# Gate and up projections: the bank Y begins with a copy of the bank X made by ScalarE; first tiles, roots and units with sums of W in another order

## The chip, the cores and the metric

One core of a Trainium2 chip. The core has TensorE (PE, matrix products into eight PSUM banks; PEld is its loading of weights), VectorE (DVE), ScalarE (ACT), GpSimd (POOL), and queues of transfers (all of them issued by SyncE, SP). Each engine works through its own list of instructions in the order in which the program was written for it, and waits at an instruction until its operands are there and its destination is free. The metric is the time of one execution in microseconds (us); less is better.

## The reference

A pre-norm block: Fourier mixing as two matrix products, and a gated feed-forward part. One batch, S = 2048 tokens, D = 448, F = 1792, everything fp32.

```python
def _A_ref(x, dft_seq_re, dft_seq_im, dft_hid_re, dft_hid_im):
    a = jnp.einsum("bsd,ed->bse", x, dft_hid_re)
    b = jnp.einsum("bsd,ed->bse", x, dft_hid_im)
    y = jnp.einsum("ts,bse->bte", dft_seq_re, a) - jnp.einsum("ts,bse->bte", dft_seq_im, b)
    return y
def _B_ref(x, w_gate, w_up, w_down):
    g = jnp.einsum("bsd,df->bsf", x, w_gate)
    u = jnp.einsum("bsd,df->bsf", x, w_up)
    h = _gelu(g) * u
    return jnp.einsum("bsf,fd->bsd", h, w_down)
h = x + _A_ref(_layernorm(x, axis=-1), ...)
h2 = h + _B_ref(_layernorm(h, axis=-1), ...)
```

## The kernel before

**Precision.** Every fp32 operand of a product is split into a high and a low fp16 part: ACT rounds the high part (`hi_part`, L100), DVE takes the difference (`lo_part`, L106, or L104 where nothing is scaled). Three products (high by high, high by low, low by high) then add up in PSUM. So behind each operand stands the pair "ACT high part, then DVE low part", and PE needs both.

**Fewer products.** Where it can, the kernel forms 2x2 blocks with seven products in place of eight (Strassen's and Winograd's forms). The sums of blocks that this needs are made ahead by DVE or POOL, and the results are joined on the way out of PSUM.

**Stage 1, features (to 107 us).** Sixteen tiles of 128 tokens. `x_load` reads two tiles (224 KB each); `x_stats` takes mean and variance on DVE and, in the same step, the square root on ACT (`root`, L121); `x_rstd` and `x_bias` finish the factor on DVE; `x_norm` and `x_lo` write the normalised tile in two parts `xs`. Tiles 0 to 3 are turned by PE into a PSUM tile `xT_ps` (L370, seven transposes in pieces of four and three) that ACT copies out (L371); the others by a DMA. `feature_mm` (L408) multiplies a turned tile with the hidden weights (`wh_hi`, `wh_lo`, made from four pieces `wh_raw` of 448 KB) in 11 steps of two products of 448 columns. `feature_out` empties the two banks `ab` into `b`; for tiles 10 to 15 (units 5 to 7), ACT copies to fp32 (`b32`), POOL makes sums (L448) and the split follows.

**Stage 2, sequence (to 371 us).** 8 passes, each of 8 units of W (512 KB, `seq_load`). A plain unit takes 24 products of 448 columns (L494), its split 1024 columns by 128 rows on ACT and on DVE. Units 5, 6 and 7 are "units with sums" (`S_UNITS`): 42 products of 224 columns, seven parts of W in place of four, of which four are sums that DVE makes (`seq_sums`). Pass 0 is woven into stage 1. Between the passes stand `seq_out` (L520 to L528: the four banks and x added up to h, on DVE), the moments of h, a root, the normalisation (on ACT) and the splits for stage 3; and through all passes run the sums and splits of the 14 gate/up weights (`gu_w`), which are stored for stage 3.

The order of stages 1 and 2 is a list of slots, one for each tile of features or unit of a pass; `plan(n, rank, step)` puts a step ahead of the products of slot n, and within a slot the steps go by rank. The first tiles, up to the first slot, are written out by hand.

**Stage 3, feed-forward (to 700 us).** 56 tiles `GateUp`: four groups q of 512 tokens by 14 blocks f of gate and up columns, 128 wide, each with 256 columns of moving operand. A tile makes seven products in three banks X, Y, Z (39 instructions of 256 columns, L872). Here `A`, `B`, `S`, `T` are blocks and sums of blocks of the weights and of the normalised h. X takes `A11 B11`, then `A12 B21`; Y takes `S2 T2`, then `S3 T3`, then `A22 T4`; Z takes `S1 T1`, then `S4 B22`. Y doesn't hold `A11 B11`, so ACT copies X to SBUF as `u1` (L910) before X's second product, and DVE adds it at each reading of Y:

```python
A.activation(self.u1, self.X, AF.Copy, scale=SC)
plus(self.u2, self.Y, self.u1)      # after S2 T2
plus(u3, self.Y, self.u1)           # after S3 T3
plus(c21, self.Y, self.u1)          # after A22 T4
G.tensor_mul(c21, c21, self.g1)     # POOL: times gelu of X
```

`plus` (L882) is one DVE instruction from PSUM. Two more join Z with `u3` and `u2`; the second gives `c12`, whose Gelu (`c_last`, ACT L946, then a product on POOL, L948) comes a tile later. In group 0 there is no down projection, and the tiles take X, Y, Z and the free banks `a0` to `a2` by turns; the down weights are prepared meanwhile (`down_prep`: load, sums on POOL at L198 and L201, `down_hi` on ACT, `down_lo` on DVE). From group 1 on each tile carries 21 products of 224 columns of the down projection (`dn_mm`, L815), for an earlier group's hidden values, which are summed (`dn_sums`, POOL L965 and L966 and one on DVE) and split (`dn_split`, L100 and L104 into `dn_w`) first. The banks `a0` to `a3` then hold its sums, and one bank (`ps_tr`) is free until the end. Steps that go beside a tile (normalisation of groups 2 and 3, draining of the down banks, the root of the last block of h at tile 25) hang on a table `side`, entry (tile, place).

**Stage 4, tail.** The down products of the last group (`last_mm`).

Of the kernel before, what the change touches and what calls it, by code (L numbers as in the profile page):

```python
# [13 lines left out]
P = 128  # L14
# [18 lines left out]
def kernel(  # L33
# [143 lines left out]

    def ffn_rstd(q, j):
        tag = f"h{q}_{j}"
        mv = moments[q, j]  # L180
        moments[q, j] = mv, rstd(mv, root(mv, tag), tag, const)

    def ffn_stats(q, j, h):
        for g in range(2):
            ffn_moments(q, j, h, g)
        ffn_rstd(q, j)
# [123 lines left out]
    def x_stats(*tiles):  # L310
# [6 lines left out]
        norm_x[tiles] = mv, root(mv, tag)  # L317
# [14 lines left out]
    def x_norm(i):  # L332
        mv, r, g, *nb = norm_x.pop(i)
# [11 lines left out]
        hi_part(xs[i][:, 0:D], xn)  # L345
# [17 lines left out]
    ptr = {}  # L363

    def x_turn_pe(i, k0, k1):
        if k0 == 0:
            xT_tile(i)
            ptr[i] = ps_dft.tile([P, 8, P], F16, tag="A", name=f"xT_ps{i}")
        for k in range(k0, k1):
            PE.transpose(ptr[i][:, k, :], xs[i][:, k * P : (k + 1) * P], ident)  # L370
        A.activation(xT[i][:, k0:k1, :], ptr[i][:, k0:k1, :], AF.Copy)  # L371
# [219 lines left out]
    for n, s in enumerate(S_UNITS):  # L591
        mixed.insert(1 + n * 8 // len(S_UNITS), s)
# [33 lines left out]
    for g, (p, u) in enumerate(units):  # L626
# [3 lines left out]
        plan(n - 2 if g else -3, 3, lambda p=p, u=u: seq_split(p, u))  # L630
        if g < 4:
            plan((-6, -5, 1, 2)[g], 9, lambda p=p, u=u: seq_load(p, u))
# [22 lines left out]
    for p in range(N_PASS):  # L655
# [6 lines left out]
        plan(n + 1, 5, lambda q=q, j=j: ffn_stats(q, j, hp[q, j]))  # L662
# [12 lines left out]
    x_load(0, (slice(0, 1),))  # L675
    x_load(0, (slice(1, 2),))
    for k in range(4):
        wh_load(k)
    x_load(1)
    x_load(ORDER[2])  # L680
    x_stats(0)
    x_rstd(0)
    x_norm(0)
    wh_high(0)
    x_stats(1)
    x_lo(0)
    x_turn_pe(0, 0, 4)
    wh_high(1)
    wh_high(3, G)
    x_turn_pe(0, 4, 7)  # L690
    x_rstd(1)
    x_norm(1)
    wh_high(2)
    x_lo(1)
    wh_low(3, G)
    feature_mm(0, range(6))
    x_stats(2)
    x_turn_pe(1, 0, 4)
    x_turn_pe(1, 4, 7)
    feature_mm(0, range(6, 7))  # L700
# [3 lines left out]
    wh_low(0)  # L704
# [3 lines left out]
    feature_mm(1, range(4, 7))  # L708
    x_stats(3)
    wh_low(1)  # L710
# [4 lines left out]
    a, b = tiles_of[2]  # L715
    x_stats(a, b)
    x_rstd(a, b)
    x_bias(a, b)
    feature_mm(2, range(7), "A")
# [409 lines left out]
    for t in range(N_GU):  # L1129
# [19 lines left out]
        if t > 0:  # L1149
            if q == 0:  # L1150
                prev.c12_plus()
# [106 lines left out]
```

## Time and profile before

| | |
|---|---|
| time of three executions | 736.61, 738.90, 739.53 us; median 738.9 |
| the profiled execution | 736.13 us, of which the span of the profile is 734.3 |
| TensorE's granted clock | 0.998 of full speed |
| busy: PE, DVE, ACT, POOL | 97%, 79%, 44%, 36% of the span |
| matmuls | 5800 |
| moved by DMA | 142.9 MB |

The span is the time from the first to the last instruction that the profile shows. A row of the profile's groups names line, engine and operation, then destination and sources by the program's names; a chain or a list of waits gives beside an instruction, in brackets, how long its engine had been idle before it and which instruction ended that. "Start to start" below means the step from one product's start to the next one's; 448 columns take 0.19 us and 256 columns 0.109 us that way when nothing is late, while the row's own duration (0.3 and more) counts the pipeline behind it.

### The profile page before, as it was taken

To read this page: it belongs to the slowest core of one execution; us is meant where nothing else is said; L and a number is where in the kernel's file an instruction comes from. 1 tells how busy PE (TensorE), PEld (TensorE's weight loads), DVE (VectorE), ACT (ScalarE), POOL (GpSimd) and SP (SyncE) were. 2 spreads that over 40 slices of the span, in tenths; PEclk is the share of its full clock that TensorE was granted. 3 is DMA by queue.
4 is the path that set the end of the run, shared out by engine and by line. 5 is a ranking of instruction groups with operands and counts; after the bars stand their busy time and mean duration, and the time that the engine had idled before them with its cause. 6 is when DMAs were issued, how large, how long until landed. Compare 5 with 4: busy or idle time off the path is not lost.

```text
span 734.3 us, 14677 instructions
## 1 busy us (share of the span) xinstructions
PE 712.6 (97%) x5800; PEld 560.9 (76%) x5800; DVE 577.6 (79%) x1166; ACT 322.0 (44%) x624; POOL 265.7 (36%) x294
## 2 busy tenths in 40 slices
PE   7899999999999999999999989999999999999998
PEld 4455567676656566676778869999999999999998
DVE  5767849998989899999457788788787877989730
ACT  5556545445454545344234444345444334454310
POOL 4032140000000000020018886576676776858430
PEclk9999999999999999999999999999999999999999
DMA  8363345798878889686147745655648476565401
GB/s 320 91 156 80 79 149 172 255 234 259 240 266 241 271 238 304 235 319 200 69 167 266 277 170 177 189 182 173 180 147 232 172 217 224 181 222 202 151 14 63
DMA packets 72340, 142.90 MB, mean 195 GB/s; under 512 B 41296, under 2 KB 47568, under 8 KB 72272
## 3 DMA queue, kind: packets, MB, share of 16 engines
q1 hardware_dynamic: 72272, 141.97, 60.8%
q8 instruction: 45, 0.74, 0.4%
q14 instruction: 23, 0.19, 0.1%
HBM read 112.46 MB, written 20.19 MB: 181 GB/s over the span
## 4 chain that ended last, share of the span: by engine, by line
PE 65%; DVE 19%; ACT 7%; DMA 4%; issue 4%; POOL 2%; SPq 1%; ACTq 0%; DVEq 0%; POOLq 0%
PE acc L494 19%; PE pY L872 13%; PE acc_d L815 11%; PE pX L872 8%; PE pZ L872 8%; DVE ws L106 4%; DVE xs L104 2%; ACT ws L100 2%; DMA w_dram<-gu_w 2%; DVE gu_w L106 2%; ACT b L100 2%; DMA x<-in_x_dram 1%; PE last_Z L1035 1%; PE last_X L1035 1%; PE last_tr L1035 1%
## 5 line engine op out<-in xcount | busy, mean ns | idle before, releaser
L494 PE MATMUL acc<-b,ws 128*128 128x448 f16 (+1 forms) x1968 | 281.5, 305 | 4.5 <-DVE ws L106 4.4
L494 PEld LDWEIGHTS <-ws 128*128 128x128 f16 x1968 | 189.4, 98 | 96.0 <-DVE ws L106 9.6
L872 PEld LDWEIGHTS <-gw 128*128 128x128 f16 x2067 | 201.8, 98 | 25.9 <-issue 5.0
L872 PE MATMUL pY<-hops,gw 128*128 128x256 f16 x901 | 122.7, 273 | 4.2 <-DVE u L882 3.9
L815 PE MATMUL acc_d<-wd,dn_w 128*128 128x224 f16 x882 | 105.1, 259 | 0.0
L815 PEld LDWEIGHTS <-dn_w 128*128 128x128 f16 x882 | 85.1, 98 | 2.8
L198 POOL TENSOR_TENSOR wd_s<-wd 128x448 f32<-128x448 f32 x7 | 8.0, 1144 | 217.0 <-DMA wd<-in_w_down_dram 217.0
L106 DVE SCALAR_TENSOR_TENSOR ws<-wr,ws 128x1024 f16<-128x1024 f32 (+2 forms) x88 | 74.6, 871 | 14.8 <-ACT ws L100 14.2
L100 ACT ACTIVATE ws<-wr 128x1024 f16<-128x1024 f32 (+2 forms) x88 | 63.7, 756 | 49.3 <-issue 30.3
L872 PE MATMUL pX<-hops,gw 128*128 128x256 f16 x583 | 81.0, 273 | 0.0
L872 PE MATMUL pZ<-hops,gw 128*128 128x256 f16 x583 | 79.2, 273 | 0.0
L939 POOL TENSOR_TENSOR hh<-hh,g 128x256 f32<-128x256 f32 x42 | 36.8, 876 | 100.5 <-DVE hh L882 100.5
L882 DVE SCALAR_TENSOR_TENSOR u<-pY,u 128x256 f32<-128x256 f32 x112 | 47.0, 420 | 32.0 <-ACT c L946 15.9
L408 PEld LDWEIGHTS <-xT 128*128 128x128 f16 x352 | 34.6, 99 | 34.3 <-issue 3.9
L910 ACT ACTIVATE u<-pX 128x256 f32<-128x256 f32 x56 | 21.4, 382 | 86.3 <-PE pX L872 80.7
L104 DVE TENSOR_TENSOR dn_w<-dn_s,dn_w 128x640 f16<-128x640 f32 x42 | 52.7, 1255 | 1.6 <-ACT dn_w L100 1.4
L923 ACT ACTIVATE g<-pX 128x256 f32<-128x256 f32 x56 | 21.3, 380 | 70.5 <-PE pX L872 64.8
L408 PE MATMUL ab<-wh_hi,xT 128*128 128x448 f16 x224 | 46.5, 359 | 1.7 <-DVE b L106 1.7
L100 ACT ACTIVATE ws<-wsum 128x1024 f16<-128x1024 f32 x24 | 25.3, 1053 | 45.6 <-DVE wsum L468 45.6
L966 POOL TENSOR_TENSOR dn_s<-hh 128x256 f32<-128x256 f32 x42 | 43.9, 1046 | 0.0
L948 POOL TENSOR_TENSOR hh<-hh,c 128x256 f32<-128x256 f32 x42 | 37.3, 887 | 17.4 <-ACT c L946 17.4
L965 POOL TENSOR_TENSOR dn_s<-hh 128x256 f32<-128x256 f32 x42 | 42.4, 1010 | 0.0
(130 smaller groups left out, 932.3 us busy)
## 6 DMA issues: line engine op xcount, KB each, us to landing
gw<-w_dram SPq DMA_DIRECT2D x53, 896.0 KB, 4.7
wr<-in_w_seq_dram SPq DMA_DIRECT2D x64, 512.0 KB, 4.3
w_dram<-gu_w SPq DMA_DIRECT2D x14, 896.0 KB, 7.4
gu_raw<-in_w_gu_dram SPq DMA_DIRECT2D x28, 384.0 KB, 5.3
wd<-in_w_down_dram SPq DMA_DIRECT2D x14, 448.0 KB, 4.9
hx<-in_x_dram SPq DMA_DIRECT2D x8, 448.0 KB, 6.3
h_dram<-hx SPq DMA_DIRECT2D x8, 448.0 KB, 6.4
hr<-h_dram SPq DMA_DIRECT2D x8, 448.0 KB, 5.3
```

Source lines behind the costliest of these rows:

```text
L100: A.activation(dst, src, AF.Copy, scale=scale)
L104: V.tensor_sub(dst, src, hi)
L106: V.scalar_tensor_tensor(dst, src, scale, hi, op0=ALU.mult, op1=ALU.subtract)
L408: PE.matmul(feat[i][r][:, :D], xT[i][:, kx, :], w[:, kw, r * D : (r + 1) * D], start=n == 0, stop=n == 10,)
L494: PE.matmul(banks[k][:, cols], lhs, rhs, start=k not in begun, stop=stop, skip_group_check=True)
L815: PE.matmul(acc[k // 2][:, k % 2 * HD : (k % 2 + 1) * HD], a_of(la, a), b_of(lb, b), start=first and m == 0 and k % 2 == 0, stop=last and ...
L872: PE.matmul(ps, w[:, wl, wa + ws, :], ops[:, m + ms, :], start=first and n == 0, stop=last and n == len(terms) - 1, skip_group_check=True,)
L882: V.scalar_tensor_tensor(dst, ps, SC, other, op0=ALU.mult, op1=ALU.add)
L939: G.tensor_mul(c21, c21, self.g1)
L948: G.tensor_mul(c22, c22, self.c12)
L965: G.tensor_add(s[:, 0:2], t[:, 0:2], t[:, 2:4])
L966: G.tensor_sub(s[:, 2:4], t[:, 1:4:2], t[:, 0:4:2])
```

## The change

In five parts. No product is added or taken away.

(a) First tiles: the first hidden weight is loaded ahead of the second tile of x; the scaling of `wh_hi` 1 goes to DVE, that of `wh_hi` 3 from POOL to ACT; each of the two pieces of a turned tile gets its own PSUM tile; the products, turns and splits stand in another order. The load and the split of the first unit of W are placed by hand.

(b) `x_stats` no longer takes the root; `x_root` does, one slot later and ahead of the steps of higher rank. Likewise `ffn_root` and `ffn_rstd` stand one slot behind the moments. On ACT, in the first pass, around the root of tiles 6 and 7 (`sd_x6`), before:

```order
L100 ACTIVATE xs6_545<-x6_417 128x448
L121 ACTIVATE sd_x6_594<-mv_x6_587,eps_t_79 128x2
L100 ACTIVATE b32_11_622<-ab11_0_598 128x448
L100 ACTIVATE b32_11_622<-ab11_1_599 128x448
L100 ACTIVATE b10_626<-b32_10_575 128x1568
L100 ACTIVATE b11_664<-b32_11_622 128x1568
```
After:

```order
L100 ACTIVATE xs6_549<-x6_421 128x448
L100 ACTIVATE b32_11_624<-ab11_0_600 128x448
L100 ACTIVATE b32_11_624<-ab11_1_601 128x448
L121 ACTIVATE sd_x6_628<-mv_x6_591,eps_t_79 128x2
L100 ACTIVATE b10_630<-b32_10_579 128x1568
L100 ACTIVATE b11_668<-b32_11_624 128x1568
```
`ab11` to `b32_11` is the emptying of tile 11's two banks; it stood behind the root and stands ahead of it now. `xs6` is the high part of tile 6, `b10` and `b11` are the splits.

(c) Units with sums come at places 2, 5 and 7 of a pass, counted from 0, in place of 1, 3 and 6: the order of the units was 0, 5, 1, 6, 2, 3, 7, 4 and is 0, 1, 5, 2, 3, 6, 4, 7. On DVE, at the start of pass 2, around the moments of the second block of h (`st_h0_1`, `mv_h0_1`), before:

```order
L175 BN_STATS st_h0_1_0_1809<-hx1_1475 128x6
L176 BN_AGGR mv_h0_1_1808<-st_h0_1_0_1809 128x2
L175 BN_STATS st_h0_1_1_1812<-hx1_1475 128x6
L176 BN_AGGR mv_h0_1_1808<-st_h0_1_1_1812 128x2
L128 RECIPROCAL r_h0_1_1817<-sd_h0_1_1815 128x2
L129 TENSOR_SCALAR r_h0_1_1817<-mv_h0_1_1808 128x2
L130 TENSOR_TENSOR r_h0_1_1817<-r_h0_1_1817 128x2
L131 TENSOR_TENSOR r_h0_1_1817<-r_h0_1_1817 128x2
L132 SCALAR_TENSOR_TENSOR r_h0_1_1817<-r_h0_1_1817 128x2
L106 SCALAR_TENSOR_TENSOR gu_w10_1766<-gu_s10_1716,gu_w10_1766 128x512 x2
L106 SCALAR_TENSOR_TENSOR ws2_2_1875<-wr2_2_1662,ws2_2_1875 128x1024
```
After:

```order
L175 BN_STATS st_h0_1_0_1805<-hx1_1449 128x6
L176 BN_AGGR mv_h0_1_1804<-st_h0_1_0_1805 128x2
L175 BN_STATS st_h0_1_1_1808<-hx1_1449 128x6
L176 BN_AGGR mv_h0_1_1804<-st_h0_1_1_1808 128x2
L106 SCALAR_TENSOR_TENSOR gu_w10_1766<-gu_s10_1698,gu_w10_1766 128x512 x2
L106 SCALAR_TENSOR_TENSOR ws2_3_1847<-wr2_3_1662,ws2_3_1847 128x1024
L128 RECIPROCAL r_h0_1_1850<-sd_h0_1_1845 128x2
L129 TENSOR_SCALAR r_h0_1_1850<-mv_h0_1_1804 128x2
L130 TENSOR_TENSOR r_h0_1_1850<-r_h0_1_1850 128x2
L131 TENSOR_TENSOR r_h0_1_1850<-r_h0_1_1850 128x2
L132 SCALAR_TENSOR_TENSOR r_h0_1_1850<-r_h0_1_1850 128x2
```
Between the moments and the factor that needs the root (L128) stand now a low part of a gate/up weight (`gu_w10`) and of a plain unit (`ws2_3`); before, that low part of `gu_w10` and the next plain unit's (`ws2_2`) came behind it.

(d) Gate/up. After `A11 B11`, ACT copies X into the bank Y (`x_open`), and `S2 T2`, `S3 T3` and `A22 T4` add onto it. So `u2` and `u3` are plain scaled copies on ACT, and the last reading of Y is one DVE instruction that multiplies with `g1`, without POOL. Odd tiles of the later groups take `ps_tr` for Y; X of the next tile is begun inside the present one. `dn_sums` of the second block comes two tiles earlier, and the first `dn_split` behind tile 12's additions. On ACT, in tiles 12 and 13, before:

```order
L946 ACTIVATE c12_11_4870<-c12_11_4870 128x256
L100 ACTIVATE dn_w0_4874<-hh0_4101 128x256
L100 ACTIVATE dn_w0_4874<-dn_s0_4742 128x640
L923 ACTIVATE g1_12_4890<-pX_12_4828 128x256
L910 ACTIVATE u1_13_4909<-pX_13_4895 128x256
L946 ACTIVATE c12_12_4939<-c12_12_4939 128x256
L923 ACTIVATE g1_13_4958<-pX_13_4895 128x256
L910 ACTIVATE u1_14_4977<-pX_14_4963 128x256
```
After:

```order
L946 ACTIVATE g1_12_4860<-pX_12_4798 128x256
L932 ACTIVATE pY_13_4869<-pX_13_4862 128x256
L970 ACTIVATE c12_11_4844<-c12_11_4844 128x256
L951 ACTIVATE u3_12_4879<-pY_12_4805 128x256
L937 ACTIVATE u2_13_4895<-pY_13_4869 128x256
L100 ACTIVATE dn_w0_4910<-hh0_4111 128x256
L100 ACTIVATE dn_w0_4910<-dn_s0_4778 128x640
L946 ACTIVATE g1_13_4927<-pX_13_4862 128x256
L932 ACTIVATE pY_14_4936<-pX_14_4929 128x256
L970 ACTIVATE c12_12_4908<-c12_12_4908 128x256
```
`u1` is gone; `pY_13<-pX_13` and `pY_14<-pX_14` are the copies of X, and `u2`, `u3` are new here. The first split of the down projection (`dn_w0`) stood ahead of `g1_12` and stands now behind `u2_13`.

(e) The root of the last block of h stays at tile 25, and its factor moves to tile 27. The banks of the last products come in another order.

The diff, cut to its core:

```diff
@@ roots, first tiles
+    def ffn_root(q, j):
+        moments[q, j] = moments[q, j], root(moments[q, j], f"h{q}_{j}")
...
-        norm_x[tiles] = mv, root(mv, tag)
+        norm_x[tiles] = mv
+
+    def x_root(*tiles):
+        norm_x[tiles] = norm_x[tiles], root(norm_x[tiles], f"x{tiles[0]}")
...
-            ptr[i] = ps_dft.tile([P, 8, P], F16, tag="A", name=f"xT_ps{i}")
+        t = ps_dft.tile([P, 8, P], F16, tag="A", name=f"xT_ps{i}_{k0}")
...
@@ slots
-    for n, s in enumerate(S_UNITS):
-        mixed.insert(1 + n * 8 // len(S_UNITS), s)
+    for n, s in zip((2, 5, 7), S_UNITS):
+        mixed.insert(n, s)
...
+                plan(n - 6, 2, lambda i=i, j=i2: x_root(i, j))
...
-        plan(n + 1, 5, lambda q=q, j=j: ffn_stats(q, j, hp[q, j]))
+        for g in range(2):
+            plan(n + 1, 5, lambda q=q, j=j, g=g: ffn_moments(q, j, hp[q, j], g))
+        plan(n + 2, 2, lambda q=q, j=j: ffn_root(q, j))
+        plan(n + 2, 5, lambda q=q, j=j: ffn_rstd(q, j))
...
@@ first tiles, by hand
     x_load(0, (slice(0, 1),))
+    wh_load(0)
     x_load(0, (slice(1, 2),))
...
+    seq_load(0, ORDER[0])
...
-    x_norm(0)
+    x_norm_v(0)
     wh_high(0)
+    x_high(0)
...
-    wh_high(1)
-    wh_high(3, G)
+    wh_high(1, V)
...
-    feature_mm(0, range(7, 11))
-    feature_out(0)
-    feature_mm(1, range(7, 9))
-    x_turn_pe(3, 0, 4)
-    x_turn_pe(3, 4, 7)
-    feature_mm(1, range(9, 11))
+    x_turn_pe(3, 0, 4)
+    x_turn_pe(3, 4, 7)
+    feature_mm(0, range(8, 11))
...
+    feature_out(0)
...
+    feature_mm(1, range(8, 11))
...
@@ class GateUp
+            self.banks = [(ps_dn, f"a{k}") for k in range(3)] if self.q == 0 and odd else [(ps_gu, k) for k in "XYZ"]
+            if self.q and odd:
+                self.banks[1] = ps_tr, "tr"
...
-    def open(self):
-            self.mul(self.Y, "S2", "T2", True)
-            A.activation(self.u1, self.X, AF.Copy, scale=SC)
-            plus(self.u2, self.Y, self.u1)
+        def x_open(self):
+            self.X = self.bank(0)
             self.mul(self.X, "A11", "B11", True)
+            self.Y = self.bank(1)
+            A.activation(self.Y, self.X, AF.Copy)
+
+        def y_open(self):
+            self.mul(self.Y, "S2", "T2", False)
             self.u2 = ftile("u2", 2, f"u2_{self.name}")
+            A.activation(self.u2, self.Y, AF.Copy, scale=SC)
...
-            plus(u3, self.Y, self.u1)
+            A.activation(u3, self.Y, AF.Copy, scale=SC)
             plus(self.hidden(1), self.Z, u3)
...
-            plus(c21, self.Y, self.u1)
-            G.tensor_mul(c21, c21, self.g1)
+            V.scalar_tensor_tensor(self.hidden(0), self.Y, SC, self.g1, op0=ALU.mult, op1=ALU.mult)
...
@@ the tiles
-        if t in (NF - 4, NF - 1):
-            dn_sums(int(t == NF - 1))
+        if t in (NF - 4, NF - 3):
+            dn_sums(t - NF + 4)
...
-    at(side, (25, 4), lambda: ffn_rstd(NB - 1, 1))
+    at(side, (25, 4), lambda: ffn_root(NB - 1, 1))
+    at(side, (27, 1), lambda: ffn_rstd(NB - 1, 1))
...
         if q == 0:
+            cur.x_close()
+            nxt.x_open()
+            if prev:
+                prev.c_last()
+            cur.y_mid()
+            nxt.z_open()
+            nxt.y_open()
+            cur.y_close()
+            cur.z_close()
             dn_ahead(t)
...
+        else:
+            do(t, 0)
+            prev.c_last()
+            cur.x_close()
+            if t > NF:
+                cur.z_open()
+            if d + 1 < 6 * NC:
+                dn_split(d + 1)
+            dn_mm(d, range(0, 8))
+            cur.y_mid()
+            dn_ahead(t)
+            dn_mm(d, range(8, 18))
+            if nxt:
+                nxt.x_open()
+            do(t, 1)
+            do(t, 4)
+            cur.y_close()
+            cur.z_close()
+            dn_mm(d, range(18, 21))
+            do(t, 5)
+            if nxt:
+                nxt.y_open()
...
```

More of the change, by code (lines that the diff above doesn't have):

```diff
@@ L176, in ffn_moments @@
         V.bn_aggr(moments[q, j][:, g, :], st)
+    def ffn_root(q, j):
+        moments[q, j] = moments[q, j], root(moments[q, j], f"h{q}_{j}")
     def ffn_rstd(q, j):
[L179 to L186, printed above, removed]
+        mv, sd = moments[q, j]
+        moments[q, j] = mv, rstd(mv, sd, f"h{q}_{j}", const)
     wd32, wd_s = {}, {}
@@ L707 @@
     x_turn_pe(2, 4, 7)
[L708 removed]
+    feature_mm(1, range(4, 8))
     x_stats(3)
[L710 removed]
+    x_root(3)
     wh_low(2)
```

117 lines of the change are left out of this document (53 added, 64 removed).

## The prediction

> **What bounds the kernel now.** First the page's totals, then the waits of TensorE (PE), then the stretches in which they fall.
>
> ```profile
> span 734.3 us, 14677 instructions
> PE 712.6 (97%) x5800; PEld 560.9 (76%) x5800; DVE 577.6 (79%) x1166; ACT 322.0 (44%) x624; POOL 265.7 (36%) x294
> PE xT_ps L370 <- ACT xT L371: 5.8, 4, 2.3
> PE pY L872 <- DVE u L882: 4.5, 4, 2.3
> PE acc L494 <- DVE ws L106: 4.4, 10, 0.7
> 107.47 34.25 PE acc L494 x243
> 376.05 1.20 PE pZ L872 x11
> 600.00:640.00 40.00, 40.00 (x385) 37.20 (x384) 32.40 (x61) 16.48 (x40) 29.16 (x34) 1.00 0.59 203
> ```
>
> The second line is busy time by engine. The next three are PE's waits (sum, times, longest); then come two dense pieces of the chain and one stretch (length; busy of PE, PEld, DVE, ACT, POOL; clock; DMA). PE is the bound, and the change leaves its products as they are in number and size. So nothing can be won but PE's gaps, some 18 us behind the first 14, and the rows say where they are not: from 600 to 640 PE issues 385 products in 40 us without a hole, and 11 gate/up products take 1.20 (0.109 each). A gate/up tile has 39 of them, 4.26 us.
>
> **The change part by part.** The sum is made against the profiled execution: 736.13 us, 1.8 more than its span. The median of the runs, 738.9, is 0.38% above it, and I scale by that at the end.
>
> *(a) First tiles.*
>
> ```profile
> x<-in_x_dram SPq DMA_DIRECT2D x2, 224.0 KB, 2.7
> wh_raw<-in_w_hid_dram SPq DMA_DIRECT2D x4, 448.0 KB, 6.8
> 7.48 0.95 ACT L100 ACTIVATE wh_hi<-wh_raw 128x896 f16<-128x896 f32 x1 [0.97 <-DMA wh_raw<-in_w_hid_dram]
> 15.00 1.08 DVE L106 SCALAR_TENSOR_TENSOR wh_lo<-wh_raw,wh_hi 128x896 f16<-128x896 f32 x1
> 22.22 0.69 DVE L104 TENSOR_TENSOR xs<-x,xs 128x64 f16<-128x64 f32 x2 [0.64 <-ACT xs L100]
> 23.40 0.39 PE L370 MATMUL xT_ps<-ident,xs 128*128 128x128 f16 x4
> 24.63 0.96 ACT L100 ACTIVATE b<-ab 128x448 f16<-128x448 f32 x2
> 26.13 0.33 PE L370 MATMUL xT_ps<-ident,xs 128*128 128x128 f16 x3 [2.34 <-ACT xT L371]
> 32.72 3.57 PE L494 MATMUL acc<-b,ws 128*128 128x448 f16 x18
> ```
>
> At 26.13 PE has waited 2.34: the last three transposes of tile 3 share a PSUM tile with the first four, whose copy stands on ACT behind both copies of `b` (24.63). Now they have their own tile, and the copies stand ahead of `b`. Against this, `wh_hi` 0 stands ahead of tile 0's high part on ACT, and the second half of x queues behind 448 KB. That weight landed at 7.48; I let it land at 6.7 and the half of x at 7.3. DVE gets one scaling of `wh_hi` more: no row has it; a low part of that size takes 1.08 and half of it is the other end; I take 1.0, since the low part is the same read with one input more. I follow DVE's queue from there (moments 0.85, low part 0.7, scaling 1.0, and so on): tile 3's low part ends at 22.7 as now (22.22 and 0.69), its transposes start at 22.8, and behind them PE has only work that is ready: 42 products by 0.19 and seven transposes, 8.3. The first sequence product moves from 32.72 to 31.1: **-1.6**. Ends: -2.2 (the weights land as fast as the first x halves) and +0.5 (tile 2 comes 2 us late). The load of the first `wr`, two issues earlier on SP, costs nothing: its split is not due before 28.
>
> *(b) Roots in the first pass.*
>
> ```profile
> 49.23 0.29 ACT L121 ACTIVATE sd_x<-mv_x,eps_t 128x2 f32<-128x2 f32 x1 [2.71 <-DVE mv_x L316]
> 54.54 1.51 ACT L100 ACTIVATE b<-b 128x1568 f16<-128x1568 f32 x1 [2.75 <-POOL b L448]
> 58.40 1.15 DVE L106 SCALAR_TENSOR_TENSOR b<-ab,b 128x448 f16<-128x448 f32 x2
> 59.07 0.35 PE L408 MATMUL ab<-wh_hi,xT 128*128 128x448 f16 x1 [0.46 <-DVE b L106]
> 63.19 0.29 ACT L121 ACTIVATE sd_x<-mv_x,eps_t 128x2 f32<-128x2 f32 x1 [3.76 <-DVE mv_x L316]
> 64.63 0.35 PE L408 MATMUL ab<-wh_hi,xT 128*128 128x448 f16 x1 [0.89 <-DVE b L106]
> ```
>
> Twice ACT sits 2.71 and 3.76 in front of a root that DVE's moments aren't ready for, with the emptying of a feature bank behind it: POOL's sums start late, ACT's split of tile 11 waits 2.75 for them, and the bank that PE wants at 58.5 is free at 59.0. Start to start PE loses 0.96 there and 1.40 at 63.4. Now the bank is emptied ahead of the root (ACT's order, above): tile 11's sums start 3 us earlier, and the bank of tile 4 is free some 2 us earlier, ahead of PE even if PE is 1.6 early by (a). For the second, DVE's moments still stand ahead of its low part of tile 5; I leave 0.5. **-1.8**, from -2.4 to -0.5.
>
> *(c) Passes 2 to 5.*
>
> ```profile
> 181.64:218.61 36.97, 35.47 (x249) 23.50 (x247) 33.40 (x70) 18.11 (x31) 0.00 (x0) 1.00 0.82 254
> DVE ws L106 <- ACT ws L100: 2.6, 2, 2.4
> DVE r_h L128 <- ACT sd_h L121: 0.4, 1, 0.4
> 187.22 21.84 PE L494 MATMUL acc<-b,ws 128*128 128x448 f16 x156 [0.34 <-DVE ws L106]
> 195.20 0.62 DVE L521 SCALAR_TENSOR_TENSOR hx<-acc,hx 128x448 f32<-128x448 f32 x1
> ```
>
> The first row is one pass, the next two are DVE's waits in it. A dense pass is 246 products: 34.25/243 by 246, 34.7 us. This one takes 36.97, and DVE's own account is 33.4 busy, 3.0 waiting, and gaps: here DVE is the bound. It begins a pass's sums at 195.20, where PE, 22 products by 0.19 behind 187.22, had ended the pass before at 191.4: 3.8 late. Three such passes lose 2.1 to 2.2 each, about 6.3.
> The work is the same after. What goes is the wait for the root (0.4), since the next low parts now stand between moments and reciprocal, and the 0.2 ahead of one split: 36.4 a pass, 1.7 over dense. The 2.4 stays: the normalisation on ACT (1.41) and a high part still stand between the bias and the next low part on DVE. With units with sums at places 2, 5 and 7 instead of 1, 3 and 6, DVE enters the first heavy pass in time (the sums of pass 0 began 1.0 late, and now 3.6 us of split and sums stand behind them), and the tightest unit is the last, with 1.9 of slack against 1.7 now. Lateness of 2.2 into pass 2, then 1.6 to 1.7 more in each: losses of 0.4, 1.4 and 1.4, 3.2 in place of 6.3. **-3.1**, from -5.0 (the 2.4 filled too) to -1.0 (the tightest unit has no slack).
>
> *(d) Gate/up, first group.*
>
> ```profile
> 423.95 1.14 ACT L100 ACTIVATE wd<-wd_s 128x1120 f16<-128x1120 f32 x1 [1.38 <-POOL wd_s L201]
> 426.11 0.72 ACT L100 ACTIVATE dn_w<-dn_s 128x640 f16<-128x640 f32 x1
> 428.10 0.71 PE L872 MATMUL pY<-hops,gw 128*128 128x256 f16 x5 [1.38 <-DVE u L882]
> 437.50 0.74 ACT L100 ACTIVATE dn_w<-dn_s 128x640 f16<-128x640 f32 x1 [1.27 <-POOL dn_s L966]
> 439.48 0.70 PE L872 MATMUL pY<-hops,gw 128*128 128x256 f16 x5 [2.29 <-DVE u L882]
> L939 POOL TENSOR_TENSOR hh<-hh,g x42: 721/729/1806, 376.7 to 611.1; 128x256 f32<-128x256 f32 x42
> L910 ACT ACTIVATE u<-pX 128x256 f32<-128x256 f32 x56 | 21.4, 382 | 86.3 <-PE pX L872 80.7
> ```
>
> At 426 and 437 the down projection's first splits (`dn_w`) sit on ACT and DVE ahead of `u3`, which PE waits for: 1.54 and 2.45 start to start, 4.2 with a small one behind. A tile now needs three additions on DVE instead of five (2 by 0.42 less), no product of `g1` on POOL (0.73 to 1.8 less), and two more copies on ACT (0.38 each by L910; the one from PSUM into PSUM has no row and lies between 0.36 and 0.42, the rows of that size). The first `dn_w` split stands behind all of tile 12's additions, and the second sums are taken two tiles earlier.
> The new waits: PE's `S2 T2` needs the copy of X in Y. In this group X ends, `S3 T3` and `S1 T1` follow (12 by 0.109, 1.31), and the copy needs 0.2 to start and 0.38: 0.7 to spare. What can eat that is ACT's queue: the split of `wd_s` (1.14) waits for POOL, whose sums (2.9) wait for DVE's low part of the block before, now behind `c12` at the tile's end. Added up, it ends 1.76 into the next tile; the copy behind it is ready at 2.46, and PE wants it at 2.50. No stall, but no slack: in six tiles I allow 0.1 each, and 0.25 where tile 13's addition stands behind the last low part. 4.2 becomes 0.7: **-3.5**, from -4.2 to -2.0.
> In the later groups PE stands dense (600 to 640), and a tile has 6.27. The copy has 0.8 to spare there, `u3` 1.0, `u2` 1.4, the drain's copies 0.1 behind `u2`; DVE drops from 32.4 of 40 by 0.84 a tile. Nothing to win, nothing lost.
>
> *(e) Table switches.*
>
> ```profile
> 371.33 1.28 ACT L1128 ACT_TABLE_LOAD   x1
> 373.38 0.82 PE L872 MATMUL pY<-hops,gu_w 128*128 128x256 f16 x6 [0.63 <-DVE u L882]
> 508.33 1.28 ACT L121 ACT_TABLE_LOAD   x1
> 509.62 0.30 ACT L121 ACTIVATE sd_h<-mv_h,eps_t 128x2 f32<-128x2 f32 x1
> 511.26 1.28 ACT L946 ACT_TABLE_LOAD   x1
> ```
>
> At 373.38 PE waits for DVE, still at the last pass's sums when `u2` is due (0.79 start to start). `u2` is ACT's now, but the load of the Gelu table stands ahead of tile 1's copy: 0.35 left, **-0.4** (0 to -0.8). The root of the last block at tile 25 makes two loads in the middle of gate/up, and PE loses 0.43 and 0.39 behind them, through DVE. The reciprocal now stands two tiles later. On ACT, load and root (1.58) fit between the copy's end and `u2`; the load back, 1.28, ends with `u3` 0.4 ahead of need: 0.1 left, **-0.7** (-0.8 to +0.5).
> The Trainium skill speaks against this term: "ScalarE: Activation LUTs", section "What ACT_TABLE_LOAD costs", puts a switch to another set at 1.28 of load and 1.38 of drain. The trace agrees with the load (1283 ns) and shows no drain: the root runs at 509.62, 1.29 behind its load's start. By the page's 2.66 two switches would put `u3` 2.3 behind its need, and the sum would be 2.3 worse.
>
> Sum: 1.6 + 1.8 + 3.1 + 3.5 + 0.4 + 0.7 = 11.1. 736.13 - 11.1 = 725.0; by 1.0038, 728.
>
> **The rivals.**
> *Only gate/up pays.* DVE is the bound in (c), and its work is unchanged; what PE gains in (a) and (b) it may lose at 106.9, where DVE's split follows a 6.2 us store, and in (c). For it: PE's waits name DVE in (b) and (c). Against: the 0.4 and the ACT orders are plain. Then 4.6 are won: 734.
> *ACT becomes the bound (slower).* Place: the copy of X ahead of `S2 T2`, 42 times in the later groups. It decides from a lateness of 0.8 plus 0.35 a tile (14.7 us over 42 tiles; 11.1 to lose and 3.7 more). At 0.5 a tile: 728 + 21 = 749. For it: PE now waits on a strict queue. Against: ACT is busy 16.48 of 40 there, and 0.76 a tile brings it to 21.
> *The half of x costs what the transposes gain.* If it lands 1.5 later than I take, DVE's queue moves with it and (a) is +0.5: 730.
> *Switches cost 2.66.* The load and a drain of its length: 2.3 at tile 25: 730.5.
>
> **How the numbers follow.** Forecast 0.55, only gate/up 0.20, ACT the bound 0.06, the half of x 0.13, slow switches 0.06. The forecast's own range, from all lower ends (15.4) to half the gain, is 723.5 to 733. With the rivals on its side, 723 to 735.5; what is left out is mostly ACT as the bound. Half a per cent, 3.7 us, is about what a measurement can tell from no change. Faster: 0.55 and most of the others but one, 0.84; same, 0.10, mainly from only gate/up; slower 0.06.
>
> **What would show it.** (a) The first sequence product near 31, no wait of PE for `xT` above 1 after 20 us. (b) No root's wait ahead of the feature banks; F12's first product without a gap. (c) Passes at about 36.2, with no DVE wait for a root; one stall a pass, at its last unit. (d) No PE wait above 0.3 between 376 and 446; POOL without the `g1` products, DVE near 27 in 40 later. (e) At tile 25 no gap above 0.2. Wrong would be a row of PE's waits that names ACT's copy into Y with more than 3 us, or a pass still at 36.9.

## The result, and the profile after

The changed kernel takes 730.63 us in the median (729.41 to 730.93, 4 runs), the kernel before 737.75 (736.44 to 739.53, 4 runs): ratio 0.9899, 95% interval 0.987 to 0.9927. It is faster by 7.1 us. Forecast were 728.0 and 10.9 less. The profiled executions, 736.13 and 730.44, are 5.7 apart, and the sum of the prediction (11.1) is held against these.

Totals of the page after, then TensorE's waits (engine and line, what ended the wait: sum, times, longest):

```profile
span 728.7 us, 14540 instructions
PE 713.2 (98%) x5800; PEld 561.3 (77%) x5800; DVE 516.4 (71%) x1055; ACT 359.2 (49%) x736; POOL 207.2 (28%) x237
PE pX L893 <- DMA gw<-w_dram: 3.2, 4, 1.7
PE acc L498 <- DVE ws L106: 3.0, 8, 0.7
PE xT_ps L374 <- DVE xs L104: 2.1, 2, 1.9
PE xT_ps L374 <- ACT xs L100: 1.1, 1, 1.1
```

The waits for `u` (4.5) and for `ab` (1.7) are gone, and so is the one for tile 3's transposes. At the top stands one that the page before doesn't have: X of a gate/up tile waits for the tile's weights, a transfer. No row names ACT's copy into Y. Waits for `ws` went from 4.4 to 3.0.

To see where the time came from, I read off four starts of products in both traces: the first into `acc`, the last into `ab`, the first into `pX` and the first of the tail (into a `last_` bank). What lies between is a stage, and its length holds all waits in it; the tail is taken to the start of the last product:

| stage | before | after | change | forecast |
|---|---|---|---|---|
| (a) to the first sequence product | 32.72 | 32.01 | -0.7 | -1.6 |
| (b) from there to the last feature product | 73.78 | 71.63 | -2.15 | -1.8 |
| (c) passes, from there to gate/up | 263.57 | 261.75 | -1.8 | -3.1 |
| (d, e) gate/up and down | 328.85 | 327.85 | -1.0 | -4.6 |
| tail | 32.1 | 32.1 | 0 | 0 |

(b) came as forecast. (a) and (c) brought about half, and gate/up, the main part of the change, brought one in place of 4.6.

How far one pair of profiles can be trusted, the profiles of the experiments below tell, since each of them leaves some stages alone. (b) is firm: 73.75 to 73.78 in four profiles with the old order, 71.63 to 71.86 in the eight with first tiles and roots as changed. So is (c): 263.57 to 263.68 in three, 260.69 to 261.88 in five. The 0.7 of (a) is not: the first sequence product comes at 31.60 to 32.75 in four profiles with the old first tiles and at 31.57 to 34.04 in those eight. Nor is the 1.0 of gate/up: its stage, as changed, takes 327.3 to 330.8 in seven profiles, on both sides of 328.85.

### The profile page after: what moved, and what is told of

Its sections match the earlier page's. It is cut to its first block, busy times and chain, and to the rows that moved or that the text cites. A ratio compares the mean times of both kernels' runs of the same rounds, so it can differ in the third digit from the quotient of the medians.

```text
span 728.7 us, 14540 instructions
## 1 busy us (share of the span) xinstructions
PE 713.2 (98%) x5800; PEld 561.3 (77%) x5800; DVE 516.4 (71%) x1055; ACT 359.2 (49%) x736; POOL 207.2 (28%) x237
## 4 chain that ended last, share of the span: by engine, by line
PE 67%; DVE 16%; DMA 8%; ACT 6%; issue 2%; SPq 1%; DVEq 0%; ACTq 0%
PE acc L498 22%; PE pY L893 13%; PE acc_d L835 11%; PE pZ L893 8%; PE pX L893 8%; DVE ws L106 4%; DMA gw<-w_dram 3%; DVE xs L104 2%; DMA w_dram<-gu_w 2%; DMA gu_raw<-in_w_gu_dram 2%; ACT b L100 1%; ACT ws L100 1%; DVE gu_w L106 1%; PE last_Z L1059 1%; PE last_X L1059 1%
## 5 line engine op out<-in xcount | busy, mean ns | idle before, releaser
L893 PE MATMUL pZ<-hops,gw 128*128 128x256 f16 x583 | 81.0, 273 | 0.4 <-DVE hh L903 0.3
L972 POOL TENSOR_TENSOR hh<-hh,c 128x256 f32<-128x256 f32 x42 | 31.3, 745 | 142.6 <-ACT c L970 142.6
L104 DVE TENSOR_TENSOR dn_w<-hh,dn_w 128x256 f16<-128x256 f32 x42 | 20.0, 476 | 53.4 <-ACT dn_w L100 53.4
L990 POOL TENSOR_TENSOR dn_s<-hh 128x256 f32<-128x256 f32 x42 | 52.4, 1247 | 0.0
L104 DVE TENSOR_TENSOR dn_w<-dn_s,dn_w 128x640 f16<-128x640 f32 x42 | 46.5, 1107 | 6.1 <-ACT dn_w L100 4.9
L937 ACT ACTIVATE u<-pY 128x256 f32<-128x256 f32 x56 | 21.4, 382 | 57.7 <-PE pY L893 57.6
L932 ACT ACTIVATE pY<-pX 128x256 f32<-128x256 f32 x56 | 20.6, 369 | 50.9 <-PE pX L893 50.9
L989 POOL TENSOR_TENSOR dn_s<-hh 128x256 f32<-128x256 f32 x42 | 37.7, 897 | 0.0
L962 DVE SCALAR_TENSOR_TENSOR hh<-pY,g 128x256 f32<-128x256 f32 x42 | 17.7, 420 | 23.9 <-PE pY L893 23.9
```

The lines of the kernel that those rows point to most:

```text
L104: V.tensor_sub(dst, src, hi)
L893: PE.matmul(ps, w[:, wl, wa + ws, :], ops[:, m + ms, :], start=first and n == 0, stop=last and n == len(terms) - 1, skip_group_check=True,)
L932: A.activation(self.Y, self.X, AF.Copy)
L937: A.activation(self.u2, self.Y, AF.Copy, scale=SC)
L972: G.tensor_mul(c22, c22, self.c12)
L989: G.tensor_add(s[:, 0:2], t[:, 0:2], t[:, 2:4])
```

## The experiments

Four questions: did gate/up gain nothing, and are late weights the reason; what is left in the first tiles; which edit moved the passes; and what holds the passes now. Each kernel has its ratio to the kernel before, run beside it on the same chip. (b) and (e) were not run alone; they are read from the profiles.

**Gate/up without the rest.** The kernel before, with the edits to `GateUp`, its steps and the root at tile 25 only:

```diff
 before.py
+ x_open, y_open, x_close, y_mid, y_close, z_close and the steps that call them
+ ffn_root(3, 1) at (25, 4), its factor at (27, 1)
```

> The kernel before with the change of gate/up alone (copy of X into Y, its steps, the root at tile 25); first tiles, roots and places as before. Theory (gate/up won nothing in its first group): the waits for u of 4.2 us there go, weights come late in their place by about 3.9, and 0.5 each is left from the Gelu table and the root at tile 25: 1.0 under the kernel before, 736.7. Rival (the late weights come from the earlier passes' order, not from gate/up's own): X waits for weights for under 1 us, and 4 to 5 are won, 733.

Measured: 737.12 (0.9989, 0.9973 to 1.0006), no difference. PE's waits from 371 to 446 us, first of the kernel before, then of this one:

```profile
PE pY L872 <- DVE u L882: 4.3, 3, 2.3
```

```profile
PE pX L876 <- DMA gw<-w_dram: 5.6, 3, 2.2
```

One wait has taken the place of another, so the gain was lost within gate/up's own change and not through the earlier stages. Its stage takes 330.14.

**A fourth buffer for weights, on the changed kernel, and on that one.** Three buffers hold the weights, and the load for tile t+2 starts when tile t-1 has ended. Before, X of that tile was begun 39 + 17 products after that start (6.1 us at 0.109 each); now it is begun 39 + 5 after it (4.8), because X comes ahead of the twelve products `S3 T3` and `S1 T1`. The transfers in both profiles, from 370 to 426 us, minimum, median and longest:

```profile
DMA to landing us min/median/max: 4.5/4.7/6.0
```

```profile
DMA to landing us min/median/max: 4.5/4.8/6.5
```

The first (before) fits under 6.1, the longest just so; the second (after) exceeds 4.8 half of the time, and where a load was late the trace shows the stall. Such a stall on PE in the changed kernel, and the first product after it:

```profile
402.64 0.71 PE L893 MATMUL pX<-hops,gw 128*128 128x256 f16 x5
405.08 0.83 PE L893 MATMUL pX<-hops,gw 128*128 128x256 f16 x6 [1.74 <-DMA gw<-w_dram]
```

Start to start such places lose 0.91, 1.90, 0.39 and 0.65 in the changed kernel, 3.85 in all.

```diff
+    gwx = fpool.tile([P, 4, 28 * P], F16, tag="hh", bufs=2, name="gwx")
 def gw_load(t):
+    if t < NF:
+        gw[t] = gwx[:, t // 4] if t % 4 == 3 else w_tile(f"gw{t}", ring if t % 4 < 2 else ring3)
...
-        if 0 < t < N_GU - 2:
+        if t < NF - 3:
+            gw_load(t + 3)
+        elif NF - 3 < t < N_GU - 2:
             gw_load(t + 2)
```

> The changed kernel with a fourth buffer for gate/up weights in the first group only (tiles 3, 7 and 11, in a buffer of the hidden values that is free until tile 14); each load starts one tile (4.26 us) earlier and is as large as before. Theory (window): a load of 4.5 to 6.5 us now has 9.0 from its start to X's need, in place of 4.8, so PE waits for no weights between 376 and 425: 3.85 us go, about 726.8. Rival (transfer rate): the first group moves 896 KB each 4.26 us and 448 KB each two tiles, which is as fast as it goes; the loads run into one another and the same 3.9 is waited, at other tiles: 730.5.

Measured: 726.78 (0.9835, 0.9821 to 0.9849). From 371 to 446 us one wait is left, and the loads from 370 to 426 took no less time than before, rather more:

```profile
PE pZ L893 <- DVE hh L903: 0.3, 1, 0.3
DMA to landing us min/median/max: 4.5/5.2/9.1
```

So the transfers were not too slow, they were started too late for a need that the change had put 1.3 us earlier. And the same buffer under gate/up alone:

> The kernel before with the change of gate/up alone and the fourth weight buffer in the first group. Alone, that change gained nothing (737.1 beside 737.6), with 6.1 us of waits for weights in its profile. If they were all that hid the gain, those waits go, the 4.2 of u are gone as well, and 0.5 each stays from the Gelu table and the root at tile 25: 5 to 6 us under the kernel before, about 733. If the copy of X on ACT sets PE's pace as well, waits that name it stand between 376 and 446 and the gain stays below 3.

Measured: 731.02 (0.9905, 0.9888 to 0.9922), 6.9 under the kernel before. From 371 to 446 us the list of PE's waits again has one row:

```profile
PE pZ L876 <- DVE hh L886: 0.3, 1, 0.3
```

With its weights in time the change of gate/up is worth what it was forecast to be, 4.6, and a bit more: its stage takes 323.94 in place of 328.85, 4.9 less. (That includes the 0.5 each at the Gelu table and at tile 25; the 6.9 of the total is more than the stage holds, and the profile shows no other stage shorter.) No wait names the copy of X.

**The window made wider in another way.** X of the next tile behind `S3 T3`, six products later:

```diff
             cur.x_close()
-            nxt.x_open()
             if prev:
                 prev.c_last()
             cur.y_mid()
+            nxt.x_open()
```

> The changed kernel; in the first group the next tile's X is begun behind the present tile's S3 T3, six products (0.65 us) later than changed, with loads and buffers as changed. Theory (window): each wait for weights gets 0.65 shorter: 0.91, 1.90, 0.39 and 0.65 become 0.3, 1.25, 0 and 0, 1.5 in place of 3.85, time 728.3. Against it: the copy of X into Y then has 0.65 of products ahead of S2 T2 and needs 0.58, behind u3 on ACT; if PE waits for the copy in each tile by 0.2 or more, 2.6 and more come back and the time is 730.5 or higher.

Measured: 729.36 (0.9882, 0.9866 to 0.9897). PE's waits from 371 to 446 us:

```profile
PE pY L893 <- ACT pY L932: 0.9, 3, 0.3
PE pX L893 <- DMA gw<-w_dram: 0.8, 2, 0.6
```

Both halves of the expectation came: start to start the weights cost 0.30, 0.72 and 0.43 (1.45; 1.5 expected), and the copy into Y, with six products ahead of `S2 T2` in place of twelve, costs 0.18, 0.48, 0.48 and 0.25. This is the wait that the prediction feared, and it shows that the twelve products which hide the copy are the same twelve that the weights had as slack.

**The load in two pieces.** This was meant to test the same and didn't:

```diff
+        for o in (slice(0, 2), slice(2, 14)):
+            nc.sync.dma_start(dst[:, :, o], src[:, :, o])
```

> The changed kernel; each gate/up weight tile (gw, 896 KB) is loaded in two pieces, the two blocks that X's first product reads (128 KB) first, the other 12 behind them. Theory (window): the load starts when the tile three before has ended, and X of a tile now starts 12 products (1.3 us) earlier than before, so the 4.6 us load is late for X in four tiles (3.85 us in all, longest 1.90). With the first blocks landing early, what is late is the rest, needed 1.3 us later: the waits between 380 and 425 fall from 3.85 to 0.6 or less, and the time by 3 us, to about 727.5. Rival (transfer rate): the first group moves as much as the DMA engines can, so the same time is lost, at Z or Y in place of X: waits stay near 3.9, time 730.5.

Measured: 729.04 (0.9882, 0.9863 to 0.9901), in the noise of the changed kernel. Waits from 371 to 446 us, and the transfers of both pieces:

```profile
PE pZ L893 <- DMA gw<-w_dram: 3.9, 4, 1.8
DMA to landing us min/median/max: 2.4/4.5/7.4
```

The waits moved to Z and their sum did not fall (3.2 at X in the changed kernel), as the transfer-rate rival said. But the edit changed the load itself: the second piece, issued 0.57 behind the first, landed up to 7.4 us after its own issue, later than a whole load did (6.5). The fourth buffer, which leaves the load alone, decides against that rival.

**First tiles: POOL beside DVE.** From 14 to 18 us in the changed kernel, DVE, then POOL:

```profile
14.41 2.75 DVE L106 SCALAR_TENSOR_TENSOR wh_lo<-wh_raw,wh_hi 128x896 f16<-128x896 f32 x1
17.09 0.68 DVE L104 TENSOR_TENSOR xs<-x,xs 128x64 f16<-128x64 f32 x2
14.33 1.89 POOL L400 TENSOR_TENSOR wh_lo<-wh_raw,wh_hi 64x896 f16<-64x896 f32 x1
```

The low part of a hidden weight takes 2.75 here. The prediction had priced this form at 1.08 by a row where POOL did something else.

```diff
-    wh_low(3, G)
...
     x_lo(3)
+    wh_low(3)
```

> The changed kernel; the low part of the fourth hidden weight (wh_lo 3, 64 rows) is made by DVE behind tile 3's low part in place of POOL at 11 to 16 us. Theory (DVE slowed beside POOL): wh_lo 1 on DVE took 2.75 us at 14.4 while POOL ran, against 1.08 for the same form alone; without POOL it takes 1.1, the low part of tile 2 comes 1.6 earlier, PE's wait of 1.86 before the turn of tile 2 nearly goes, and the first sequence product moves from 32.0 to about 30.5: 729. Rival (DVE's queue as such is the limit): the 1.1 us that DVE now takes over itself comes back before 32, and the first sequence product stays within 0.4 of 32.0: 730.5.

Measured: 728.87 (0.988, 0.9861 to 0.9899). DVE from 14 to 18 us, and the first sequence product:

```profile
13.53 1.08 DVE L106 SCALAR_TENSOR_TENSOR wh_lo<-wh_raw,wh_hi 128x896 f16<-128x896 f32 x1
14.53 0.68 DVE L104 TENSOR_TENSOR xs<-x,xs 128x64 f16<-128x64 f32 x2
27.94 1.22 PE L498 MATMUL acc<-b,ws 128*128 128x448 f16 x5
```

2.75 is 1.08 again, and the first sequence product comes at 27.94 in place of 32.01, 4.07 earlier. The one instruction accounts for 1.67 of that. It also started 0.9 earlier, at 13.53 in place of 14.41, behind a second hidden weight that had landed at 6.82 in place of 7.67, which the edit doesn't touch. And 1.4 is TensorE's clock. The first products of tile 2, and the stretch around them (the last three figures are granted clock, DMA share and GB/s), in the changed kernel and in this one:

```profile
18.13 2.45 PE L412 MATMUL ab<-wh_hi,xT 128*128 128x448 f16 x6
15.00:20.00 5.00, 2.74 (x13) 1.32 (x14) 4.90 (x11) 1.37 (x4) 1.22 (x1) 0.75 0.63 231
```

```profile
15.45 1.30 PE L412 MATMUL ab<-wh_hi,xT 128*128 128x448 f16 x6
15.00:20.00 5.00, 4.76 (x34) 2.73 (x33) 4.22 (x13) 1.86 (x4) 0.00 (x0) 1.00 0.54 202
```

The eight products from 18.13 take 2.89, 0.37 from one to the next; the same eight take 1.51 from 15.45, 0.19 from one to the next. The granted clock sorts all profiles with the new first tiles: three have a granted clock of 0.91 from 10 to 30 us and the first sequence product at 31.57 to 32.47, five have 0.83 to 0.86 and 33.19 to 34.04, and the two without POOL's low part have 1.00. Whether the edit keeps the clock up, for instance because PE waits less ahead of the turn of tile 2 (1.86 in the changed kernel, 0.18 here), isn't shown.

Of the 4.1 about 3 are left at the last feature product (100.61, from 103.64). In the profiled execution almost none shows (729.81 beside 730.44): the gate/up stage lost 330.83 - 327.85 = 3.0. Start to start 1.2 of that are later weights (5.1 in place of 3.85) and the rest is again the clock, which fell to half from 420.9 to 424.4, behind a wait for weights of 2.1:

```profile
420.00:425.00 5.00, 4.14 (x23) 3.09 (x24) 0.50 (x2) 1.37 (x5) 2.06 (x3) 0.66 0.40 158
```

The Trainium skill has this in "SBUF — State Buffer", section "Who interferes with whom": a DVE instruction with two SBUF inputs contends with a GpSimd instruction that reads SBUF, and whoever issues second is blocked until the other has finished. By that rule DVE, second at 14.41, would begin at 16.22, when POOL's 1.89 are over, and end at 17.3 with its 1.08; it ended at 17.16. The trace agrees. Where POOL's instruction has one operand the trace does not bear the rule out: in the kernel before, the row at 15.00 that the prediction went by began as the second, beside a POOL scaling that ran from 13.90 to 16.35, and took its 1.08.

**Passes: the places.**

```diff
-    for n, s in zip((2, 5, 7), S_UNITS):
+    for n, s in zip((1, 3, 6), S_UNITS):
```

> The changed kernel with the units with sums at places 1, 3 and 6 as before, the roots as changed. Theory: of the 1.5 us that passes 1 to 7 gained, the places bring most, since with them the first heavy pass is entered in time: losses between 107 and 370 rise from 4.9 to about 6, time +1.1, 731.7. Rival (the roots bring it): losses stay within 0.4 of 4.9, 730.6; the places only moved the losses from pass 2 to passes 3 and 4.

Measured: 731.6 (0.9922, 0.9901 to 0.9943). The passes take 262.07, 0.2 above what kernels with the changed passes show (260.69 to 261.88 in five profiles), and PE's wait for `ws` is the same:

```profile
PE acc L498 <- DVE ws L106: 2.9, 7, 0.7
```

The places bring 0.2 to 1.4 by the profile; the interval of the total can't tell it from none.

**Passes: the root of h in one slot with its moments.**

```diff
-        plan(n + 2, 2, lambda q=q, j=j: ffn_root(q, j))
-        plan(n + 2, 5, lambda q=q, j=j: ffn_rstd(q, j))
+        plan(n + 1, 5, lambda q=q, j=j: ffn_root(q, j), lambda q=q, j=j: ffn_rstd(q, j))
```

> The changed kernel with the moments, the root and the factor of h in one slot again (passes 1 to 7); places of the units as changed. With the old places and the new roots the losses between 107 and 370 were 4.9 us, as in the changed kernel, against 6.4 before. Theory (the roots bring the 1.5): DVE waits 0.4 for each root again, and the losses rise to 6.2 or more: 732. Rival (either of the two edits suffices, or other things moved): they stay below 5.3.

Measured: 733.39 (0.9929, 0.9907 to 0.995). PE's wait from 107 to 368 us, and DVE's from 181 to 293:

```profile
PE acc L498 <- DVE ws L106: 3.6, 7, 0.7
DVE r_h L128 <- ACT sd_h L121: 1.1, 3, 0.4
```

DVE waits for the root again, and the passes take 263.13, near the 263.57 of the kernel before. Start to start PE's losses in the passes are 6.1, where the changed kernel has 4.7 and the kernel before 6.4. So most of (c) came from the root being taken a slot later.

**Passes: what remains.** In the changed kernel, pass 3 from 217.90 (length; busy of PE, PEld, DVE, ACT, POOL), and what happens on ACT and DVE at the normalisation of pass 2:

```profile
217.90:255.30 37.40, 35.61 (x247) 23.42 (x246) 33.23 (x70) 17.99 (x31) 0.00 (x0) 1.00 0.84 251
204.84 1.41 ACT L216 ACTIVATE xn_h<-hx,nb_h,r_h 128x448 f32<-128x448 f32 x2 [3.54 <-DVE nb_h L214]
206.16 0.92 ACT L100 ACTIVATE ws<-wr 128x256 f16<-128x256 f32 x2
206.59 0.42 DVE L106 SCALAR_TENSOR_TENSOR ws<-wr,ws 128x256 f16<-128x256 f32 x1 [1.79 <-ACT ws L100]
```

ACT, idle for 3.54, waits for the bias of the normalisation and has the high part of a unit behind it, for which DVE then waits 1.79.

```diff
-            plan(n + 2, 6, lambda q=q, j=j: ffn_norm_act(q, j, hp[q, j]))
+            plan(n + 3, 4, lambda q=q, j=j: ffn_norm_act(q, j, hp[q, j]))
```

> The changed kernel; the normalisation of h on ACT (1.41 us, passes 1 to 4) comes a slot later, behind the high parts of the next unit with sums. Theory (ACT's order holds DVE up): DVE's wait of 1.79 for that high part, once in each of passes 2 and 3, goes, and with it 1.8 of lateness in each: losses between 107 and 370 fall from 4.9 to about 2, 727.8. Rival (DVE's own work, 33 to 34 of 34.7 us in a pass, is the limit): the sums of the normalised h wait for it instead, losses stay above 4, 730.5.

Measured: 728.41 (0.9855, 0.9832 to 0.9878). From 180 to 300 us PE issues 843 products in one piece, and two stretches of 35 us have DVE as busy as before:

```profile
179.76 120.43 PE L498 MATMUL acc<-b,ws 128*128 128x448 f16 x843
180.00:215.00 35.00, 35.00 (x249) 23.95 (x248) 33.94 (x72) 18.88 (x31) 0.00 (x0) 1.00 0.87 267
215.00:250.00 35.00, 35.00 (x249) 23.93 (x248) 31.96 (x67) 17.52 (x30) 0.00 (x0) 1.00 0.92 268
```

The passes take 257.12: all 4.6 are gone with one step put behind another on ACT, more than the 3 that was expected. DVE's work didn't bound the passes; its waiting behind ACT's order did: the changed kernel has that 1.79 three times (at 170.22, 206.59 and 244.11), this one nowhere. (DVE's other waits for ACT, most of them behind 285 us, stay, and PE loses nothing by them.) The total moved by 2.2 only, since the gate/up stage of this kernel took 329.17, weights late by 4.9, and its first sequence product came 1.2 later, in a profile of a granted clock of 0.83 from 10 to 30 us. The same line in the kernel before:

> The kernel before with the late normalisation alone; places and roots as before. If ACT's order (the normalisation ahead of the high part) was the main loss of the passes, the losses between 107 and 370 fall from 6.4 to 2 or less, time 738.8 to 734. If DVE's work in the old order was (roots and places), they stay above 4.5, 737 or more.

Measured: 732.69 (0.9928, 0.9909 to 0.9947). PE's wait from 107 to 368 us falls from 4.4 to

```profile
PE acc L494 <- DVE ws L106: 1.3, 2, 0.7
```

and the passes take 258.88, 4.7 less, with old roots and old places. This one line, alone, is worth most of what the whole change brought.

**Passes: the sums of gate/up weights a slot later.**

```diff
-        plan(n, 7, lambda f=f: gu[f].sums())
+        plan(n + 1, 6, lambda f=f: gu[f].sums())
```

> The changed kernel; the sums of a gate/up weight on DVE come a slot later, just ahead of its split. Theory: in pass 3 DVE waits 1.42 for a weight that lands 7.0 us behind its issue, at 226.6, with the last sums of pass 2 behind it; a slot later the weight is there, and the loss of that pass falls from 2.7 to 1.3: 729.2. Rival: the sums, 1.7 us, only stand in the way of the next low part; losses stay at 4.9 or grow: 730.6 or more.

Measured: 733.07 (0.9926, 0.99 to 0.9953), and the passes take 262.88, 1.1 more. DVE no longer waits for the transfer, and PE waits more for `ws` (from 107 to 368 us):

```profile
PE acc L498 <- DVE ws L106: 3.8, 5, 1.0
```

This is the way that the rival forecast, the sums standing ahead of the next low part; that they are what delays it is read from these waits and not tested further.

**All three repairs.** Fourth buffer, `wh_lo` 3 on DVE, late normalisation:

> The changed kernel with the fourth weight buffer in the first group, wh_lo 3 on DVE, and the late normalisation together. If the three losses are independent, the changed kernel's 730.6 loses 3.85 (weights), 3.0 (first sequence products) and 4.7 (passes): 719. If one of them was only moved on by the others (weights of gate/up stored too late, a bank that isn't free), 723 or more.

Measured: 719.64 (0.9747, 0.9729 to 0.9765), 2.5% under the kernel before and 11 us under the changed one.

```profile
span 717.6 us, 14537 instructions
PE 709.7 (99%) x5800; PEld 562.1 (78%) x5800; DVE 515.1 (72%) x1056; ACT 359.3 (50%) x736; POOL 202.7 (28%) x235
28.53 0.54 PE L498 MATMUL acc<-b,ws 128*128 128x448 f16 x2
```

The stages add up: the first sequence product at 28.53 (3.5 earlier than in the changed kernel, at a granted clock of 1.00), from there to the last feature product 72.67 (1.0 more), passes 257.07 (4.7 less), gate/up 323.96 (3.9 less). So the three repairs don't undo one another. With four buffers the gate/up stage takes 323.94, 323.98 and 323.96 in three kernels; with three buffers, and loads and steps as changed, 327.3 to 330.8 in seven.

## Why the prediction was right, and where its terms were wrong

The time lay in the range and on the forecast's side; the size of the gain was 7.1 in place of 10.9. Two of the five terms, (b) and (e), came as worked out, (c) in part; that the total stayed in the range in spite of (d) owes something to the width of the range.

*(d), the term that failed.* The step "the new waits" listed ACT's copy and DVE's additions and allowed enough for them: the waits for `u` went, no wait names the copy, DVE fell from 32.40 to 24.44 of 40 us (near 27 was forecast) and ACT rose from 16.48 to 21.53 (600 to 640 us):

```profile
600.00:640.00 40.00, 40.00 (x386) 37.16 (x384) 24.44 (x50) 21.53 (x55) 23.29 (x28) 1.00 0.60 214
```

What it left out is the transfer. It said that X is begun earlier and never asked what X reads. The number was there: a load takes 4.7 us in the median, and 44 products by 0.109 are 4.8. It cost 3.85 of the 4.2 won in the first group, and the range of the term (-4.2 to -2.0) didn't reach to that. This is also why none of the rivals describes what happened, though "only gate/up pays" came out upside down: (b) and (c) paid, gate/up hardly.

*(a)* was forecast at 1.6 and measured at 0.7, within its range, but by luck of this pair of profiles: over all of them (above) no gain is shown. Tile 3's wait is gone as said. In its place PE waits 1.9 for tile 2's low part, which stood behind a `wh_lo` of 2.75 us; the prediction followed DVE's queue with 1.08. A row of the same form at 2.0 stood in the trace before as well (17.35, beside POOL's low part), and the shorter one was taken. The sum also took every product at full clock, and eight of them cost 1.4 more. Two terms erred the other way: the first weight landed at 4.69 and the half of x at 5.59, where 6.7 and 7.3 were taken.

*(b)* as forecast: 2.15 for 1.8. The bank is emptied ahead of the root and tile 11's sums start in time.

*(c)* was forecast at 3.1 and measured at 1.8 (1.7 to 3.0 over the profiles above). The wait for the root went, as said. The places, on which the 0.4 for the first heavy pass rested, brought little; pass 2 did lose only 0.33, but passes 3 and 4 lost 2.7 and 1.7 where 1.4 each was forecast, and in pass 3 DVE stood 1.42 waiting for a gate/up weight, which wasn't in the sum. By the prediction's own sign of being wrong, "a pass still at 36.9", this term failed: pass 3 takes 37.40 (the row from 217.90). That "DVE is the bound" in these passes was wrong: the prediction saw the 2.4 that DVE waits behind ACT, took it as given, and named its removal only as the lower end of the range (-5.0). The late normalisation shows that, in the changed kernel, this kind of wait was the whole loss.

*(e)* as forecast: 0.5 at 370 us for 0.4, and 0.55 at tile 25 for 0.7 (0.26 are left at 510.86, through DVE). Of ACT at tile 25:

```profile
504.36 0.37 ACT L932 ACTIVATE pY<-pX 128x256 f32<-128x256 f32 x1 [1.17 <-PE pX L893]
504.74 1.28 ACT L121 ACT_TABLE_LOAD   x1
506.04 0.29 ACT L121 ACTIVATE sd_h<-mv_h,eps_t 128x2 f32<-128x2 f32 x1
506.39 0.38 ACT L937 ACTIVATE u<-pY 128x256 f32<-128x256 f32 x1
506.79 1.28 ACT L970 ACT_TABLE_LOAD   x1
508.08 0.42 ACT L970 ACTIVATE c<-c 128x256 f32<-128x256 f32 x1
```

A switch costs its 1.28: each load starts where the instruction ahead ends, and the next one starts where it ends. The 1.38 of drain that the Trainium skill adds in "ScalarE: Activation LUTs", section "What ACT_TABLE_LOAD costs", shows in neither of these two switches, and the rival built on them is out.

So the sign and the range were right with a sum that was not: 4.6 of its 11.1 stood for gate/up, which gave 1.0.

## What to carry to other kernels

When a change moves a product earlier, price everything that the product reads, the weights' transfer first: from the release of the buffer to the new need, against the longest transfer in the trace and not the median. When an engine is 95% busy and still waits for another, look at the order on that other engine before calling it the bound: one step put behind the high part on ACT freed 4.6 us, where a reordering of the whole pass freed 1.8. And a stage that waits for transfers can vary by itself, here from 327.3 to 330.2 us at full clock between kernels with the same code in it, and by 0.04 once the transfers were early, which is enough to hide what an earlier stage gains: repair it first, or measure by stage.

## What the runs showed of the hardware that was not expected

- Loads of 896 KB took 4.5 to 6.5 us (370 to 426 us in the changed kernel), and 6.7 to 9.1 where the fourth buffer let two be issued within 0.4 us of each other; a load cut into 128 KB and 768 KB had its second part land up to 7.4 us after its issue.
- A DVE instruction with two operands in SBUF stood still while POOL ran one with two operands of its own: 2.75 us for 1.08, the difference being what was left of POOL's 1.89. Beside POOL's one-operand scaling it took its 1.08, both when it had started first (10.85, changed kernel) and when it came second (15.00, kernel before).
- TensorE's granted clock fell to half for 3.4 us or 6.9 us at a time, and products then came at half the rate (0.37 us each in place of 0.19). In three places this began within 0.2 us of the end of a wait of PE of 1.9 to 2.3 us (17.5 in the changed kernel, 420.9 with `wh_lo` 3 on DVE, 433.7 in the kernel before with the late normalisation); the wait of 2.29 that ended at 439.48 in the kernel before was followed by none. What decides it stays open.
- ACT copies 128x256 from one PSUM bank into another in 0.37 us, no more than from PSUM to SBUF (0.38).
